# A gated mix of memory attention and a token MLP on one core: DMA issue moved off POOL, half of the LN apply moved to ACT, instruction order changed

## The chip, the cores and the metric

The kernel runs on one core of a Trainium2 chip. The time is the device time of one execution in microseconds (us).

Engines: PE (matmuls; PEld is its weight load), DVE (VectorE), ACT (ScalarE), POOL (GpSimd), SP (SyncE, which here only issues DMAs). "DMA on POOL" means that POOL's instruction stream starts the transfer.

## The reference

```python
x = A_x                                   # [1, 2048, 448] bf16, 16 heads of 28
g = sigmoid((x * gate_w).sum(-1))
# a: four stripes of 512 tokens; causal softmax attention inside a stripe, plus a
#    linear-attention memory (phi(q) M / phi(q) z) of the earlier stripes; then @ wo
# b: h = layernorm(x); u = gelu(h^T w1 + b1); y = u w2 + b2, mixing over the tokens
return g * a + (1 - g) * b                # [1, 2048, 448]
```

## The kernel before

A helper records every operation with the buffers that it reads and writes and derives the semaphore waits from that. One list gives the order; each engine executes its own entries of it, in that order. An entry is `what@engine`, with buffer or bank numbers after the engine (`P01`: PSUM banks 4 and 5).

```python
# the head of the list in the kernel before, line breaks added
warm@P ldwk.0@A dve0@D id@G ldx.0@S ldx.1@S ldwq.0@A ldsm@G ldwk.1@S acttab@A ldwq.1@S ldwv.0@S
trx.0.2@P xw.0@D  ... seven trx.0, seven trx.1 ...  setup@G ... ldwv.1@S ... ex.1@A ... ex.0@D pad.0@D ex.3@A
xtd.1@S ex.2@D tb@A bn.1@D pair.0.1@P01 pad.1@A bn.3@D bet@D pair.0.0@P23 eq.0.1@A btr@P1 ek.0.1@D ...
```

What the entries do, as far as the argument needs it:

```python
NWARM = 7                       # warm: dummy 128x512 matmuls at the start

def setup(eng, u):              # POOL
    op("POOL", lambda e: e.memset(mhalf[:], -0.5), writes=[R_mhalf])
    op("POOL", lambda e: e.memset(maskg[:], 0.0), writes=[R_maskg])
    op("POOL", lambda e: e.memset(oAM[:], 0.0), writes=R_o)          # 128 x 3072 bf16

def xw(eng, u, h):              # DVE: 64 columns of x copied behind the row, for the transposes
    op("DVE", lambda e: e.tensor_copy(x0[:, r, D:512], x0[:, r, 0:64]), ...)

# ldsm: five small loads (gate_w twice, b1, b2, beta).  ldx: x.  ldwk/ldwq/ldwv: weights, in halves.
# trx: PE transposes x of stripe 0.  ex: their copies out of PSUM.  pad: repack of wk and wq.
# pair.s.g: K and Q projection of stripe s, head group g (14 matmuls).  eq/ek: their evictions.
# v.p: V projection, its last column is the gate.  gt: tanh of the gate, on ACT.
# btr: transpose of gate_w, b1, b2 on PE; gcp, b1c, b2c: its copies.  tb, bet: sigmoid(beta), head masks.
# xtd, xtc, ldx.2: transposed and plain loads for stripe 1.
# sc/exp/mask/pv: scores, exponential, causal mask, P times V.  u, y: the two token matmuls of the MLP.
# bn, lnc: LN statistics.

def lna(eng, u, t):             # LN apply, on DVE
    op(eng, lambda e: e.tensor_scalar(xtile(t)[:, 0, :], xtile(t)[:, 0, :], rstd[:, t : t + 1],
                                      nmr[:, t : t + 1], op0=ALU.mult, op1=ALU.add), ...)
```

The softmax here doesn't subtract the row's maximum and nothing guards it: scores larger than these inputs give would overflow.

## Time and profile before

| | before |
|---|---|
| time, median of the first three runs | 190.9 us (189.59 to 190.95) |
| span of the profiled run | 188.6 us |
| PE busy | 175.7 us |
| PE idle before 33 us / in 33-67 us / in 67-186.1 us / after | 5.7 / 4.35 / 0.4 / 2.5 us |

The page's first part, two lines: the span, and PE's busy time, share and instructions.

```profile
span 188.6 us, 3618 instructions
...
PE 175.7 (93%) x1470; PEld 81.9 (43%) x1470; DVE 140.2 (74%) x271; ACT 122.2 (65%) x110; POOL 57.8 (31%) x94
```

The stretches view of the kernel before: each line is a stretch of time, its length, then busy time of each engine in it.

```profile
0.00:11.00 11.00, 6.33 (x35) 3.85 (x36) 7.42 (x11) 3.29 (x6) 6.75 (x14) 1.00 0.94 186
11.00:33.00 22.00, 20.99 (x191) 9.14 (x192) 20.07 (x55) 15.22 (x23) 9.70 (x28) 1.00 1.10 248
33.00:67.00 34.00, 29.65 (x276) 12.82 (x275) 30.39 (x57) 27.86 (x26) 13.27 (x25) 1.00 0.61 131
67.00:100.00 33.00, 32.91 (x312) 13.87 (x311) 26.35 (x47) 27.05 (x23) 10.65 (x11) 1.00 0.33 83
```

The first busy number is PE's, the third is DVE's. PE is nearly full from 67 us on; in 33-67 us it lacks 4.35 us while DVE is busy for 30.4 of 34 us.

The timeline of the kernel before at the start, in order of time (start, length, engine, line, operation; in brackets the idle time before it and what ended it):

```profile
1.45 1.30 POOL L356 DMA_DIRECT2D t<-in_gate_w_dram  x2
...
3.75 0.58 POOL L356 DMA_DIRECT2D t<-in_A_beta_dram  x1
...
4.12 3.49 DVE L508 COPY t<-t 128x128 bf16<-128x128 bf16 x2
...
4.27 1.27 PE L517 MATMUL t<-t 128*128 128x128 bf16 x10
...
4.84 2.68 POOL L443 MEMSET t<- 128x3072 bf16 x1
7.63 1.84 PEld L517 LDWEIGHTS t<-t 128*128 128x128 bf16 x18 [2.35 <-DVE t L508]
7.63 2.10 PE L517 MATMUL t<-t 128*128 128x128 bf16 x18 [2.08 <-DVE t L508]
...
11.00 4.62 PE L545 MATMUL t<-t 64*128 64x512 bf16 x28 [1.27 <-DVE t L366]
...
11.40 0.15 PEld L545 LDWEIGHTS t<-t 64*128 64x128 bf16 x2 [0.28 <-issue]
...
13.95 1.18 PEld L545 LDWEIGHTS t<-t 64*128 64x128 bf16 x12 [0.26 <-issue]
```

Two things are to be seen. The copies of x columns (L508) end with POOL's memset (at 7.6 and 7.52 us), and PE waits 2.08 us for them. And the first projections (L545) start slowly: until 13.95 us there is one step of weight loads in about 0.43 us, afterwards twelve loads in 1.18 us, which is one step of two in about 0.2 us. That is half the rate (the array is "cold" below; at full rate it is "warm"). The column for the granted clock (the 1.00 in the stretches) doesn't show it in this profile.

The source view of the LN apply on DVE (min/median/max ns), for its cost:

```profile
L833 DVE TENSOR_SCALAR t<-t x16: 307/386/1162, 23.3 to 46.5; 128x448 bf16<-128x448 bf16 x16
```

### The profile page before, as it was taken

To read this page: it belongs to the slowest core of one execution; us is meant where nothing else is said; L and a number is where in the kernel's file an instruction comes from. 1 tells how busy PE (TensorE), PEld (TensorE's weight loads), DVE (VectorE), ACT (ScalarE), POOL (GpSimd) and SP (SyncE) were. 2 spreads that over 40 slices of the span, in tenths; PEclk is the share of its full clock that TensorE was granted. 3 is DMA by queue.
4 is the path that set the end of the run, shared out by engine and by line. 5 is a ranking of instruction groups with operands and counts; after the bars stand their busy time and mean duration, and the time that the engine had idled before them with its cause. 6 is when DMAs were issued, how large, how long until landed. Compare 5 with 4: busy or idle time off the path is not lost.

```text
span 188.6 us, 3618 instructions
## 1 busy us (share of the span) xinstructions
PE 175.7 (93%) x1470; PEld 81.9 (43%) x1470; DVE 140.2 (74%) x271; ACT 122.2 (65%) x110; POOL 57.8 (31%) x94
## 2 busy tenths in 40 slices
PE   7578999977998799999999999999999999999994
PEld 3524444332344354444345444454444444555554
DVE  5697999997998793894996538299835998596032
ACT  3157569967796968888799956995775668401300
POOL 8501566637223133323320222301333423200000
DMA  6999999979047231572008330660534470638011
GB/s 154 212 202 266 289 200 267 153 181 264 6 133 168 37 78 33 165 215 72 0 0 222 104 95 1 197 195 0 168 103 129 123 214 25 168 95 225 27 49 50
DMA packets 50296, 24.92 MB, mean 132 GB/s; under 512 B 15016, under 2 KB 49896, under 8 KB 50280
## 3 DMA queue, kind: packets, MB, share of 16 engines
q1 hardware_dynamic: 49192, 24.23, 52.4%
q10 hardware_dynamic: 928, 0.46, 1.1%
q8 instruction: 11, 0.18, 0.4%
q0 software_dynamic: 160, 0.01, 0.1%
q14 instruction: 5, 0.04, 0.1%
HBM read 18.54 MB, written 1.84 MB: 108 GB/s over the span
## 4 chain that ended last, share of the span: by engine, by line
PE 66%; DVE 19%; POOL 4%; issue 3%; ACT 2%; DMA 2%; SPq 1%; DVEq 0%
PE t L898 21%; PE t L845 16%; PE t L545 8%; PE t L871 7%; PE t L694 4%; PE t L735 4%; PE t L570 4%; DVE t L366 3%; DMA t<-t 2%; DVE t L617 2%; DVE t L508 2%; DVE t L833 2%; POOL t L812 2%; DVE t L803 1%; DVE t L608 1%
## 5 line engine op out<-in xcount | busy, mean ns | idle before, releaser
L704 ACT ACTIVATE t<-t 128x2048 bf16<-128x2048 f32 x40 | 75.1, 1877 | 22.5 <-PE t L694 22.3
L717 POOL TENSOR_SCALAR_AFFINE_SELECT t<-t 128x1024 bf16<-128x1024 bf16 (+1 forms) x40 | 38.4, 963 | 87.6 <-ACT t L704 73.9
L845 PE MATMUL t<-t 128*128 128x448 bf16 x224 | 48.7, 354 | 1.8 <-DVE t L833 1.3
L898 PE MATMUL t<-t 128*128 128x448 bf16 (+1 forms) x238 | 45.8, 342 | 0.0
L545 PE MATMUL t<-t 64*128 64x512 bf16 x224 | 28.0, 392 | 3.4 <-DVE t L366 2.6
L898 PEld LDWEIGHTS t<-t 128*128 128x128 bf16 x238 | 22.3, 98 | 20.1 <-issue 2.5
L845 PEld LDWEIGHTS t<-t 128*128 128x128 bf16 x224 | 20.1, 98 | 24.4 <-issue 5.3
L364 ACT ACTIVATE t<-t 128x512 bf16<-128x512 f32 (+4 forms) x27 | 16.6, 636 | 12.6 <-PE t L517 5.0
L907 DVE SCALAR_TENSOR_TENSOR t<-t 128x448 bf16<-128x448 f32 (+1 forms) x17 | 11.0, 649 | 16.0 <-PE t L898 15.9
L545 PEld LDWEIGHTS t<-t 64*128 64x128 bf16 x224 | 10.6, 97 | 18.1 <-issue 4.4
L366 DVE CAST t<-t 128x512 bf16<-128x512 f32 (+1 forms) x24 | 15.4, 650 | 2.3 <-PE t L570 1.8
L694 PE MATMUL t<-t 28*128 28x512 bf16 (+3 forms) x256 | 15.8, 301 | 0.0
L871 PE MATMUL t<-t 128*128 128x448 bf16 x64 | 13.8, 353 | 0.0
L881 ACT ACTIVATE t<-t 128x448 bf16<-128x448 f32 x8 | 5.8, 722 | 11.8 <-DVE t L884 11.4
L613 ACT ACTIVATE t<-t 128x1024 bf16<-128x1024 bf16 x12 | 12.6, 1056 | 0.0
L570 PE MATMUL t<-t 64*128 64x449 bf16 x112 | 12.1, 350 | 0.0
L755 DVE STREAM_TRANSPOSE t<-t 128x512 f32<-128x512 f32 x16 | 11.0, 700 | 1.2 <-PE t L735 1.2
L735 PE MATMUL t<-t 128*32 128x512 bf16 (+3 forms) x256 | 11.1, 301 | 0.7 <-DVE t L366 0.4
L776 DVE SCALAR_TENSOR_TENSOR t<-t 128x448 bf16<-128x448 f32 x16 | 11.4, 724 | 0.2
L759 DVE STREAM_TRANSPOSE t<-t 128x512 f32<-128x512 f32 x12 | 8.4, 697 | 4.3 <-PE t L748 4.3
L795 DVE STREAM_TRANSPOSE t<-t 128x512 bf16<-128x512 bf16 x16 | 11.2, 698 | 0.1
L884 DVE TENSOR_SCALAR t<-t 128x448 bf16<-128x448 f32 x8 | 6.0, 744 | 6.8 <-PE t L871 6.7
(70 smaller groups left out, 157.8 us busy)
## 6 DMA issues: line engine op xcount, KB each, us to landing
t<-in_B_w_dram SPq DMA_DIRECT2D x7, 1024.0 KB, 6.4
t<-in_B_w_dram SPq DMA_DIRECT2D x8, 896.0 KB, 5.1
out_dram<-t SPq DMA_DIRECT2D x15, 112.0 KB, 1.7
t<-in_A_x_dram SPq DMA_DIRECT2D x3, 448.0 KB, 4.6
t<-t SPq DMA_DIRECT2D x6, 192.0 KB, 3.2
t<-in_A_wv_dram SPq DMA_DIRECT2D x2, 392.0 KB, 8.0
t<-in_A_x_dram SPq DMA_DIRECT2D x2, 224.0 KB, 3.7
t<-in_A_wo_dram SPq DMA_DIRECT2D x4, 98.0 KB
```

What stands on the lines that cost most here:

```text
L364: op("ACT", lambda e: e.activation(out, in_, ACT.Copy), reads=reads, writes=writes)
L366: op(eng, lambda e: e.tensor_copy(out, in_), reads=reads, writes=writes)
L545: last = e.matmul(bank(bb)[:, 0:512], wkq[half[h], c, 128 * hg : 128 * hg + 128], xTb[half[h], b, i, :], start=(i == 0), stop=(i == 6), sk ...
L570: last = e.matmul(bank(bs[h])[:, 0 : D + 1], xTb[half[h], b, i, k0 : k0 + 128], wvx[half[h], (LC, UC)[h][i], 0 : D + 1], start=(i == 0), s ...
L613: op("ACT", lambda e: e.activation(et[:, i, :].rearrange("p (g t) -> p g t", g=2), two(T, hp, s), ACT.Exp), reads=[RT[2 * hp][s], RT[2 * h ...
L694: last = e.matmul(bank(hl)[:, c0 : c0 + w], kT[r, hg, s * 512 + j * 128 : s * 512 + j * 128 + 128], qT[r, hg, s * 512 + 128 * j : s * 512 ...
L704: op("ACT", lambda e: e.activation(punit(i).rearrange("p (a q) -> p a q", a=4), ps[:, 0:4, :], ACT.Exp, scale=SCALE), reads=R_bank[0:4], w ...
L717: op("POOL", lambda e: e.affine_select(d, d, pattern=pat, compare_op=ALU.is_ge, fill=0.0, base=0, channel_multiplier=-1), reads=[R_P[i]], ...
L735: last = e.matmul(bank(b)[32 * hl : 32 * hl + 32, 128 * j : 512], vaug[:, 4 * s + j, 32 * h : 32 * h + 32], p4[:, hl, c0 : c0 + w], start= ...
L845: op("PE", lambda e: e.matmul(bank(b)[:, 0:D], w[:, st, (ft % 2) * 128 : (ft % 2) * 128 + 128], xtile(st)[:, 0, :], start=(st == 0), stop= ...
L871: last = e.matmul(bank(b)[:, 0:D], oT[:, hg, T * 128 : T * 128 + 128], wo_sb[:, hg, :], start=(hg == 0), stop=(hg == NHG - 1), skip_group_ ...
L898: op("PE", lambda e, b=b, f=f, c0=c0, n=n: e.matmul(bank(b)[:, 0:n], w[:, f, c : c + 128], uT[:, f, c0 : c0 + n], start=(f == 0), stop=(f ...
```

## The change

Its intent: POOL issues no DMA any more, so that its memsets come early; ACT issues the loads of wv; SP issues the small loads after x; the LN apply may run on DVE or ACT; the whole order was found anew by annealing, with instruction durations varied so that the order does not lean on exact ones. There is also one more warm-up matmul.

```diff
-NWARM = 7
+NWARM = 8
 PLAN = """
-warm@P ldwk.0@A dve0@D id@G ldx.0@S ldx.1@S ldwq.0@A ldsm@G ldwk.1@S acttab@A ldwq.1@S ldwv.0@S trx.0.2@P xw.0@D
-... setup@G trx.1.0@P ldwv.1@S ... tb@A bn.1@D pair.0.1@P01 pad.1@A bn.3@D bet@D pair.0.0@P23 eq.0.1@A btr@P1 ...
+warm@P ldwk.0@A dve0@D id@G ldx.0@S ldx.1@S ldwq.0@A setup@G ldsm@S ldwv.0@A ldwv.1@A acttab@A ldwk.1@S ldwq.1@S
+... pad.0@D tb@A bn.3@D pair.0.0@P01 bn.0@D bet@D btr@P2 eq.0.0@A ek.0.0@A pair.0.1@P31 b2c@D pad.1@A gcp@D ...
 ... (about 80 lines of order; LN applies 1,2,4,5,7,9,12,14 on ACT; two projections of stripe 2 much later)
     def lna(eng, u, t):
+        x, sc_, bi = xtile(t)[:, 0, :], rstd[:, t : t + 1], nmr[:, t : t + 1]
+        if eng == "ACT":
+            op("ACT", lambda e: e.activation(x, x, ACT.Identity, bias=bi, scale=sc_), ...)
+        else:
+            op(eng, lambda e: e.tensor_scalar(x, x, sc_, bi, op0=ALU.mult, op1=ALU.add), ...)
```

## The prediction

> **What bounds it now.** TensorE. The page's first part gives PE 175.7 us busy of a 188.6 us span. The stretches view places the 12.9 us of idle: 4.7 us before 11 us, 1.0 in 11-33, 4.35 in 33-67, 0.7 in 67-186.1, and the 2.5 us tail. After 67 us the order hardly matters; what can be won lies before.
>
> **The start.** The groups list DVE's copy of x columns (two pieces) at 3458 and 1743 ns; the timeline has them from 4.12 to 7.6 us, ending as POOL's 2.68 us memset (4.84-7.52) ends, and PE waits 2.1 us for them. [...] POOL is that late because it issues five small DMAs first (1.45-4.33 us). The first 14 column steps of the first projection take about 0.43 us each, until 13.95 us, so two projections take 4.62 us instead of about 3.2. [...]
>
> **What the change does.** POOL goes from the identity straight to its memsets (3.4 us), which should end near 4.8-5.0 us instead of 7.5. The x copies then end at 5-6 us, about 2 us earlier. The first projection should start at 9-9.3 us instead of 11.0, and nearer full rate: another 0.7-1.4 us. Against it: SP issues the small loads (about 0.6 us each, from its other issues; some 3 us), so the second halves of wk and wq leave near 5 us instead of 1.8-2.6, the x transposes about 1.5 us later, and ACT's wv loads compete. Later projections may wait briefly. Net gain by the first token-mixing matmul (32.6 us before): 2-3 us.
>
> **33-67 us.** DVE is 30.4 of 34 us busy there, and the chain of waits runs through DVE pieces from 35 to 57 us. The LN apply has median 386 ns but mean 534 and maximum 1162, again beside POOL. Eight move to ACT (about 0.55 us each, estimated from its 448-element evictions), taking about 4.3 us off DVE; two projections of stripe 2 with their evictions move later, which relieves both. Of the 4.35 us idle I expect 1.5-2.5 back. Four more output combines on DVE come late and cost nothing. PE's switches between kinds of work barely change (154 to 158 in the order).
>
> **Sum.** Gains 2-3 + 1.5-2.5 us, less about 0.5 us of new waits: 4.5 us, that is 186.3 us from 190.9. Range 183.5 to 189.6. Chances: faster by over 2% 0.60, within 2% 0.37, slower 0.03.
>
> **What would show it right.** POOL's long memset ends before 5.2 us and the x copies last under 1.5 us; the first projection starts before 9.7 us and the first two take under 4 us; PE idle before 33 us falls from 5.7 to about 3.5, in the next 34 us below 3; LN apply on DVE keeps a mean below 534 ns; PE busy falls by 1-1.5 us in total (less cold time); the rest stays PE-bound, same tail.
>
> **What would make it wrong.** DVE memsets or x copies still blocked by the earlier POOL memsets; the late wk and wq halves or stripe 1's transposes arriving after PE wants them (PE waits on the weight repack or DMA at 12-18 us); ACT becoming the limit at 20-45 us; holes in 50-100 us because filler work was spent early.

The copies end at 7.6 us as the memset does at 7.52, and the two projections take 4.62 us instead of about 3.2. The sum: 2-3 and 1.5-2.5 us, 5 us together in the middle, less 0.5 us make its 4.5 us.

Two remarks in it have these numbers in the traces. Its longest LN applies did run beside POOL: the one of 1162 ns at 44.64 us beside a mask of 44.55 to 45.68 us, the one of 1.14 us at 30.03 beside a mask of 29.95 to 31.05. That loads compete was its estimate: the DMA share was 0.94 and 1.10 in the first two stretches of before; in after the second halves of wk and wq landed 7.0 and 6.9 us after their issue, in before 5.8 us, and whether the wv loads caused that was not tested.

Two figures in it are misread: its "14 column steps" of about 0.43 us are 14 matmuls in seven pairs, 0.43 us a pair, and the stretches give 0.4 us of idle in 67-186.1 us, not 0.7.

## The result, and the profile after

| | before | after |
|---|---|---|
| time, median | 190.84 us (189.59 to 190.95, 4 runs) | 184.53 us (183.97 to 185.70, 4 runs) |
| ratio | 1 | 0.9692, 95% interval 0.9630 to 0.9753 |
| span of the profiled run | 188.6 us | 182.2 us |
| PE busy | 175.7 us | 172.7 us |
| PE idle before 33 us / in 33-67 us | 5.7 / 4.35 us | 6.3 / 0.5 us |

A ratio is the mean time of one kernel's fast runs over that of the other's of the same rounds, so it is not quite the ratio of the medians. The kernel is 3.1% faster.

The page's first part and the stretches of the kernel after:

```profile
span 182.2 us, 3611 instructions
...
PE 172.7 (95%) x1471; PEld 79.7 (44%) x1471; DVE 135.7 (74%) x268; ACT 123.9 (68%) x116; POOL 54.5 (30%) x89
...
0.00:11.00 11.00, 6.84 (x51) 3.36 (x51) 5.52 (x12) 3.20 (x6) 3.80 (x9) 1.00 0.96 190
11.00:33.00 22.00, 19.86 (x206) 8.09 (x206) 20.43 (x53) 20.93 (x30) 12.51 (x34) 1.00 1.02 215
33.00:67.00 34.00, 33.50 (x303) 14.69 (x300) 27.92 (x54) 29.01 (x30) 12.66 (x20) 1.00 0.90 182
67.00:100.00 33.00, 33.00 (x299) 14.58 (x298) 25.92 (x52) 27.84 (x27) 6.70 (x7) 1.00 0.24 65
```

The 6.4 us of span split into 3.0 us less PE busy time and 3.4 us less idle. The idle was won in 33-67 us (3.85 us). Before 33 us there is more of it than before (0.6 us). PE does the same matmuls in both kernels but for one warm-up, so busy time that vanishes is time in which the same matmuls ran slower: the transposes took 3.37 us and now take 1.89, the first two projections 4.62 and now 1.69 and 1.68.

The timeline of the kernel after, its start:

```profile
1.80 2.66 POOL L443 MEMSET t<- 128x3072 bf16 x1
...
4.10 0.41 DVE L508 COPY t<-t 128x128 bf16<-128x128 bf16 x1
4.38 0.94 PE L517 MATMUL t<-t 128*128 128x128 bf16 x14
...
5.65 0.19 DVE L508 COPY t<-t 128x128 bf16<-128x128 bf16 x1 [1.14 <-DMA t<-in_A_x_dram]
...
8.21 1.69 PE L545 MATMUL t<-t 64*128 64x512 bf16 x14 [1.58 <-DVE t L366]
10.82 0.19 PE L462 MATMUL t<-t 37*128 37x37 bf16 x1 [0.93 <-DMA t<-in_A_beta_dram]
...
11.55 1.68 PE L545 MATMUL t<-t 64*128 64x512 bf16 x14 [0.54 <-ACT t L364]
```

The memset now ends at 4.46 us; the copies take 0.6 us together; the first projection starts at 8.21 us instead of 11.0 and runs at full rate from its first step (14 matmuls in 1.69 us). But then PE waits for the small loads (beta landed at 10.8 us) and for ACT. The second projection begins at 11.55 us. So 2.8 us of an earlier start are there, and by 33 us PE has been idle for longer than before.

The LN apply after, on both engines:

```profile
L838 DVE TENSOR_SCALAR t<-t x8: 377/390/1240, 20.5 to 39.8; 128x448 bf16<-128x448 bf16 x8
...
L835 ACT ACTIVATE t<-t x8: 746/776/820, 20.9 to 39.3; 128x448 bf16<-128x448 bf16 x8
```

### The profile page after: what moved, and what is told of

It is laid out like the page before. It is cut to its first block, busy times and chain, and to the rows that moved or that the text cites. A ratio compares the mean times of both kernels' runs of the same rounds, so it can differ in the third digit from the quotient of the medians.

```text
span 182.2 us, 3611 instructions
## 1 busy us (share of the span) xinstructions
PE 172.7 (95%) x1471; PEld 79.7 (44%) x1471; DVE 135.7 (74%) x268; ACT 123.9 (68%) x116; POOL 54.5 (30%) x89
## 4 chain that ended last, share of the span: by engine, by line
PE 75%; SPq 6%; DVE 6%; ACT 5%; DMA 4%; POOL 1%; issue 1%
PE t L902 22%; PE t L849 21%; PE t L545 8%; PE t L875 7%; PE t L694 6%; SPq L356 6%; PE t L570 5%; PE t L735 4%; DMA t<-in_A_x_dram 4%; ACT t L704 3%; ACT t L835 2%; PE t L748 2%; PE t L659 1%; DVE t L366 1%; DVE t L803 1%
## 5 line engine op out<-in xcount | busy, mean ns | idle before, releaser
L545 PE MATMUL t<-t 64*128 64x512 bf16 x224 | 26.6, 377 | 3.3 <-DVE t L366 2.8
L364 ACT ACTIVATE t<-t 128x512 bf16<-128x512 f32 (+4 forms) x27 | 16.4, 644 | 5.0 <-PE t L545 2.2
L545 PEld LDWEIGHTS t<-t 64*128 64x128 bf16 x224 | 9.8, 94 | 16.9 <-DVE t L366 3.9
L885 ACT ACTIVATE t<-t 128x448 bf16<-128x448 f32 x4 | 2.9, 724 | 18.9 <-PE t L875 18.9
L755 DVE STREAM_TRANSPOSE t<-t 128x512 f32<-128x512 f32 x16 | 11.3, 709 | 5.0 <-PE t L735 5.0
L888 DVE TENSOR_SCALAR t<-t 128x448 bf16<-128x448 f32 x12 | 8.7, 728 | 6.3 <-PE t L875 6.3
L784 DVE TENSOR_TENSOR t<-t 128x448 bf16<-128x448 f32 x12 | 10.9, 911 | 0.1
L776 DVE SCALAR_TENSOR_TENSOR t<-t 128x448 bf16<-128x448 f32 x16 | 10.9, 687 | 0.1
```

What stands on the lines that cost most here:

```text
L364: op("ACT", lambda e: e.activation(out, in_, ACT.Copy), reads=reads, writes=writes)
L545: last = e.matmul(bank(bb)[:, 0:512], wkq[half[h], c, 128 * hg : 128 * hg + 128], xTb[half[h], b, i, :], start=(i == 0), stop=(i == 6), sk ...
```

## The experiments

Twelve runs were made (eleven edited kernels and the kernel after again), all with correct results. Line numbers of their profiles are mostly one lower than in the kernels that they were made from. An overview, each ratio against the kernel before in the same rounds.

| run | what it is | ratio | 95% interval |
|---|---|---|---|
| e1_memset_held | before, POOL's long memset out of the way of the x copies | 0.9903 | 0.9856-0.9949 |
| e2_new_front_old_order | new loads and start, old order and apply | 0.9974 | 0.9916-1.0033 |
| e4_old_front_new_order | old loads and start, new order and apply | 0.9855 | 0.9819-0.9892 |
| e3_apply_on_dve | after, all LN applies on DVE | 0.9710 | 0.9674-0.9745 |
| a1_after_again | after, unedited | 0.9679 | 0.9641-0.9717 |
| l1_apply_on_act_old_order | before, eight LN applies on ACT | 0.9938 | 0.9901-0.9974 |
| w16_before_sixteen_warm | before, 16 warm-up matmuls | 0.9858 | 0.9832-0.9884 |
| x16_old_front_new_order_warm | e4 with 16 warm-up matmuls | 0.9693 | 0.9671-0.9714 |
| i1_small_consumers_late | after, small loads used later | 0.9652 | 0.9615-0.9690 |
| i2_small_loads_last | i1, small loads issued later too | 0.9736 | 0.9701-0.9770 |
| i3_bet_on_pool | i1 mended, beta work on POOL | 0.9705 | 0.9669-0.9741 |
| i4_x_load_first | i3, one x load moved ahead | 0.9608 | 0.9587-0.9630 |

### Were the x copies held by POOL's memset?

```diff
 # kernel before; setup@G is moved behind pad.0@D in the list, and
-op("POOL", lambda e: e.memset(oAM[:], 0.0), writes=R_o)
+op("POOL", lambda e: e.memset(oAM[:], 0.0), reads=[R_wp[0]], writes=R_o)
```

> The kernel before, with one edit: POOL's three memsets are held back until the first weight repack on DVE has ended (a true dependence), so that none of them runs while the x columns are copied. POOL still issues the small loads. If the x copies lasted 3.4 us because POOL's long memset blocked DVE (my theory), they take under 0.7 us together, PE's wait of 2.1 us for them shrinks to at most 1.2 us (the arrival of the second x load), the first projection starts near 9 us and the time falls by 1 to 3 us. If they waited for the x loads instead (rival), they still take about 3 us and nothing moves.

The edit holds back less than this says: only the long memset waits, the two short ones still run at 4.34 to 4.93 us.

Measured: 0.9903, 189.1 us median. From the timeline of this run:

```profile
4.11 0.25 DVE L507 COPY t<-t 128x128 bf16<-128x128 bf16 x1
...
5.93 0.20 DVE L507 COPY t<-t 128x128 bf16<-128x128 bf16 x1 [1.57 <-DMA t<-in_A_x_dram]
5.96 0.96 PE L516 MATMUL t<-t 128*128 128x128 bf16 x14 [0.87 <-DMA t<-in_A_x_dram]
...
13.86 2.83 PE L544 MATMUL t<-t 64*128 64x512 bf16 x14 [0.69 <-ACT t L363]
```

The first copy takes 0.25 us instead of 3.46. The rival, that it waited for x, falls. So the long memset held the copies in this kernel; by what mechanism, the runs do not show. One thing stays open: by the records the long memset began at 4.84 us, while without it the first copy was over at 4.36 us, so its start time does not explain the hold (the profile itself calls spans on POOL rough). PE's wait was 0.87 us, within the expected 1.2, and the first projection started at 8.65 us.

The 0.9903 is not what the held copies are worth. The transposes and the first two projections of `e1` are warm (0.95 and 0.96 us for 14 each, then 3.19 us), but its third projection, at 13.86 us, and the V projection behind it are cold (2.83 us against 1.69, 2.08 against 1.50), after gaps of 1.14 and 0.69 us.

### Front and order apart

`e2` takes the kernel before and replaces only what stands ahead of the transposes:

```diff
-warm@P ldwk.0@A dve0@D id@G ldx.0@S ldx.1@S ldwq.0@A ldsm@G ldwk.1@S acttab@A ldwq.1@S ldwv.0@S ... setup@G ... ldwv.1@S
+warm@P ldwk.0@A dve0@D id@G ldx.0@S ldx.1@S ldwq.0@A setup@G ldsm@S ldwv.0@A ldwv.1@A acttab@A ldwk.1@S ldwq.1@S
-NWARM = 7
+NWARM = 8
```

`e4` is the reverse: these lines of the kernel before in the kernel after.

> The kernel before with only the loads and the start of the change: no DMA on POOL, its memsets right after the identity, wv loads on ACT, small loads on SP, eighth warm-up matmul; the order from the transposes on, and the LN apply, as before. If the front is worth what I predicted, 2 to 3 us faster than before (188 to 189 us), with the first projection near 8.3 us. If the whole gain of 6.3 us comes from the front (rival 1), 184 to 186 us. If the early start is given back in full to waits for the small loads and for the second weight halves (rival 2), within 1 us of before.

> The kernel after with the loads and the start of the kernel before (POOL issues the small loads, its memsets come last, wv on SP, seven warm-up matmuls), with the new order and the new LN apply. If the parts add up with the run that has only the new front, this is 3 to 4 us faster than before (187 to 188 us). If the new order needs the early start, it is no faster than before. The x copies should take about 3.4 us again and the first projection start near 11 us.

Measured: the new front alone gives 0.9974, not told apart from nothing. The order and the apply alone give 0.9855, 188.07 us. Together the two give 0.9692. The parts don't add: 0.3% and 1.45% against 3.1%.

The PE timelines of `e2` (first fence) and `e4` (second) tell why:

```profile
8.83 4.79 PE L544 MATMUL t<-t 64*128 64x512 bf16 x28 [2.12 <-DVE t L365]
```

```profile
10.57 3.17 PE L544 MATMUL t<-t 64*128 64x512 bf16 x14 [1.32 <-DVE t L365]
...
14.43 3.17 PE L544 MATMUL t<-t 64*128 64x512 bf16 x14 [0.67 <-ACT t L363]
```

At full rate 14 of these take 1.69 us and 28 take 3.19. In `e2` two projections took 4.79 us, in `e4` two took 3.17 us each. Both are still cold, though `e2` starts its first projection at 8.83 us. For `e4` the profile's page shows half clock outright, in its line for the granted clock (40 slices of 4.65 us, in tenths; 9 is 90% or more), with a 5 in the two slices from 9.3 to 18.6 us:

```profile
PEclk9855999999999999999999999999999999999999
```

So cold time, not the start time, looked like the missing piece. A theory from two profiles is not enough; the next runs test it.

### Cold time by itself

```diff
 # w16: the kernel before.  x16: e4 (old front, new order).  In both only:
-NWARM = 7
+NWARM = 16
```

The nine further dummy matmuls run while PE would wait for the x copies anyway: in `w16` the transposes begin at 7.74 us, and in the kernel before they resume at 7.63.

> The kernel before with sixteen warm-up matmuls instead of seven, nothing else: PE stays busy until about 6.3 us, inside the time in which it waits for the x copies anyway. If the cold stretch of before (about 2.9 us more for the transposes and the first two projections than in after) comes from PE's idle time before them, the two projections take about 3.2 us instead of 4.6 and the time falls by 1.5 to 3 us. If the cold stretch depends on the execution alone (rival), it stays within 0.7 us of before.

> The run with the old loads and the new order (188.07 us, about 4 us of cold time in its profile), with sixteen warm-up matmuls. Theory: the new front is worth little but the warm array, so this comes within 1 us of after: 184.3 to 185.6 us. Rival: the new front is worth its earlier first projection (2.4 us); then this stays 2 us or more behind after, at 186.5 us or more.

Measured: `w16` 0.9858, 188.19 us; `x16` 0.9693, 184.99 us. PE timelines of `w16` and then of `x16`:

```profile
1.31 6.59 PE L449 MATMUL t<-t 128*128 128x512 bf16 x16 [1.31 <-DVE t L927]
...
11.04 3.19 PE L545 MATMUL t<-t 64*128 64x512 bf16 x28 [1.57 <-DVE t L366]
...
15.02 1.69 PE L545 MATMUL t<-t 64*128 64x512 bf16 x14 [0.77 <-ACT t L364]
```

```profile
10.40 1.69 PE L544 MATMUL t<-t 64*128 64x512 bf16 x14 [1.58 <-DVE t L365]
...
12.78 1.69 PE L544 MATMUL t<-t 64*128 64x512 bf16 x14 [0.68 <-ACT t L363]
```

In `w16` the first projection starts no earlier than in the kernel before (11.04 against 11.00 us), and two projections take 3.19 us instead of 4.62. One constant, nine more dummy matmuls, is worth 1.4% or 2.7 us (0.0142 of 191 us). The rival, that the cold stretch depends on the execution alone, falls. The expectation missed one thing: the warm-ups ran until about 7.8 us, not 6.3, at about 0.41 us each.

The profiles place only part of the 2.7 us. Matmul by matmul, `w16` is 1.39 us ahead of the kernel before when the third projection starts (15.02 against 16.41 us), all of it from the first projection, and 1.78 us from 66 us on. The transposes, warm too (28 in 1.73 us, in before 3.37), gained nothing, since the first projection starts no earlier. The other 0.9 us is not located (the profiled `w16` is the slowest of its four).

`x16` keeps POOL's DMAs, its late memsets and the held x copies, starts its first projection 2.2 us later than after does, and is as fast as after (0.9693 against 0.9692 and, in the repeat, 0.9679). So within these intervals, and in the new order, the whole new front of the change is worth the warm array and nothing else. The new front with a warm array in the old order was not run. With a warm array the order and the apply give 0.9858 to 0.9693, that is 1.65% or about 3.1 us, and the sum of 2.7 and 3.1 us is the gain (5.9 us, 3.1% of 191).

### The LN apply

`e3` is the kernel after with the letter of eight list entries changed from A to D; `l1` is the kernel before with the new `lna` function and the same eight on ACT.

> The kernel after, with all sixteen LN applies on DVE again, order untouched. If moving half of them to ACT is what removed PE's idle time in 33-67 us (4.35 us before, 0.5 after), this is 2 to 4 us slower than after (186.5 to 188.5 us) with PE idle of over 2 us in that stretch. If the order did it (rival), it stays within 1 us of after.

> The kernel before with the same eight LN applies on ACT, order and loads untouched. If the relief of DVE by itself is worth the 1.5 to 2.5 us that I predicted for 33-67 us, 188.5 to 189.5 us. If it only helps together with the new order (which the small cost of undoing it there, about 1 us, already makes likely), within 1 us of before, since ACT then pays about 0.78 us for each and its exponentials come later.

Measured: 0.9710 and 0.9938. In the old order the move is worth 0.6% (about 1.2 us), more than nothing and less than the 1.5 to 2.5 us predicted for the relief. In the new order undoing it costs 0.2 to 0.3% (about 0.3 to 0.6 us, intervals overlapping with after's; by the medians 1.0 us, so the rival of `e3` holds narrowly). So most of the 3.1 us is the order. The stretch 33-67 us of `l1`, then of `e3`:

```profile
33.00:67.00 34.00, 31.40 (x292) 13.82 (x294) 28.31 (x54) 31.91 (x33) 14.47 (x29) 1.00 0.62 130
```

```profile
33.00:67.00 34.00, 32.80 (x299) 14.45 (x296) 28.27 (x60) 27.30 (x27) 14.34 (x24) 1.00 0.86 182
```

PE's idle time there is 4.35 us before, 2.6 with the apply alone, 1.2 with the order (and the new front) but not the apply, and 0.5 with all. The order relieves DVE there as much as the move does (28.3 us of DVE busy time in both, 30.4 before): two projections of stripe 2 with their evictions now come later. It also brings ACT's exponentials forward: the first starts at 13.62 us instead of 21.47. Both are seen in the profiles; which of the order's many moves brought the gain was not tested.

### What limits the start of the kernel after

`i1` moves the consumers of the small loads behind the second projection and gives that projection banks which it need not wait for; `i2` also issues the small loads after the second weight halves:

```diff
-... pad.0@D tb@A bn.3@D pair.0.0@P01 bn.0@D bet@D btr@P2 eq.0.0@A ek.0.0@A pair.0.1@P31 b2c@D pad.1@A gcp@D b1c@D bn.1@D bn.2@D sc.0.0@P
+... pad.0@D bn.3@D pair.0.0@P01 bn.0@D eq.0.0@A ek.0.0@A bn.1@D bn.2@D pair.0.1@P32 btr@P1 gcp@D tb@A sc.0.0@P ek.0.1@D eq.0.1@D b2c@D b1c@D bet@D pad.1@A
 # from there on PSUM banks 5 and 6 are exchanged
 # i2 only: ldsm@S stands behind ldwq.1@S
```

> The kernel after, unedited, as the anchor for the other runs of this call: 184 to 185.5 us. It also shows how much the cold time of the array changes from one execution to the next: if the cold stretch depends on the execution and not on the kernel, PE busy differs by about 1 us between this profile and the first one of after.

> The kernel after with the consumers of the small loads moved behind the second projection: PE's transpose of the biases, ACT's tanh of beta, DVE's use of both; the second projection in other PSUM banks, so that it waits for no eviction. In after, PE waits 0.93 us for the beta load and 0.54 us for ACT between the first two projections. If these waits are what ate the early start, the first V projection begins near 12.2 us instead of 13.6 and the time falls by 0.5 to 1.5 us against after. If DMA arrival of the second weight halves then binds instead (rival), PE waits move to the third projection and the time stays within 0.4 us of after.

> As the run before this, and SP issues the second halves of wk and wq before the five small loads instead of after them. If arrival of these halves (12.15 us in after) binds the second repack and with it the third projection, this is 0.3 to 1 us faster than the run before it. If the small loads then come so late that the V projection waits for the gate column, it is slower than that run.

Measured: `a1` 184.38 us median, but its profiled execution took 186.37 us; `i1` 184.43 us (0.9652, one of its six runs was slow and is left out); `i2` 185.83 us (0.9736), slower. `i1` is not told apart from after: the waits between the first two projections went, but PE then waited 1.3 us for the bias copies, so that the first V projection began at 14.00 us and not near 12.2, and 1.0 us for the gate's tanh. In `i2` beta landed at 13.2 us, PE waited 1.3 us for it, and one later projection ran cold (3.14 us). So, in this order, the small loads must stay early.

`a1` answers the question asked of it with no: its array was as warm as in the first profile (transposes 0.94 and 0.96 us, first two projections 1.68 and 1.69). Its slow execution has another cause, shown in its timeline:

```profile
22.06 1.16 DVE L803 BATCH_NORM_STATS2 t<-t 128x6 f32<-128x448 bf16 x2 [3.23 <-DMA t<-in_A_x_dram]
...
25.55 1.69 PE L545 MATMUL t<-t 64*128 64x512 bf16 x14 [2.17 <-DVE t L366]
```

DVE sat 3.23 us in front of the LN statistics, whose x tiles (the second x load) had not landed; the evictions queued behind them, and PE waited 2.17 us for an eviction. In the first profile of after DVE waited 1.0 us there.

`i3` mends what `i1` showed:

```diff
-pair.0.1@P32 btr@P1 gcp@D tb@A sc.0.0@P ek.0.1@D eq.0.1@D b2c@D b1c@D bet@D pad.1@A ... ev.2@D pke.0.0@A0 ev.3@D ... gt.1@A
+pair.0.1@P32 btr@P1 gcp@D b2c@D b1c@D tb@A sc.0.0@P ek.0.1@D eq.0.1@D pad.1@A ... lnc.0@G bet@G ... ev.2@D ev.3@D gt.1@A pke.0.0@A0
 # bet runs on POOL; the masks on POOL also wait for its last results
```

> As the run with the consumers of the small loads moved back, mended where its profile showed new waits: the three copies of the transposed biases right after it, the fourteen small beta instructions on POOL instead of DVE, the tanh of the gate before the exponential of the first key features. In that run PE waited 1.3 us for the bias copies and 1.0 us for the gate's tanh. If those waits are all that took the gain, the first V projection begins near 13 us, the fourth projection near 16.3 us instead of 17.9 to 18.4, and the time is 183 to 184 us. If stripe 1 or the LN statistics then wait for their DMAs (rival), within 0.5 us of after.

Measured: 184.98 us, 0.9705: no gain. The timeline of `i3`, PE and one line of DVE:

```profile
12.53 1.50 PE L569 MATMUL t<-t 64*128 64x449 bf16 x14
...
16.03 1.69 PE L544 MATMUL t<-t 64*128 64x512 bf16 x14
...
20.93 1.15 DVE L802 BATCH_NORM_STATS2 t<-t 128x6 f32<-128x448 bf16 x2 [2.88 <-DMA t<-in_A_x_dram]
...
24.42 1.69 PE L544 MATMUL t<-t 64*128 64x512 bf16 x14 [2.49 <-DVE t L365]
```

The V projection and the fourth projection came 1.1 and 1.9 us earlier than in after, as intended, and all of it was returned at 24.42 us: DVE had waited 2.88 us for the same x load. The rival holds.

`i4` moves that load. In `i3` SP issues it after the copies `xtc.1`, and SP waits for the transposed load before it can issue those (it stands idle from 12.35 to 14.18 us).

```diff
-pad.1@A xtc.1@S v.1@P01 lnc.0@G bet@G exp.0.0@A0 ldx.2@S
+pad.1@A ldx.2@S xtc.1@S v.1@P01 lnc.0@G bet@G exp.0.0@A0
```

> As the run with the beta instructions on POOL, and one DMA moved: SP issues the x tiles of stripe 1 (second x load) before the copies that wait for the transposes to land, where SP otherwise sits idle from 12.4 to 14.2 us. In that run DVE waited 2.9 us for these tiles (1.0 us in the first profile of after, 3.2 in its second) and PE then 2.5 us for DVE. If that load is what now limits the start, DVE's wait falls below 1 us, PE's waits in 16-26 us below 1 us in sum, and the time is 182 to 183.8 us: faster than after by 0.5 to 2 us. If the DMA queue as a whole limits it (rival), the copies of stripe 1 come later instead, PE waits for them, and the time stays at 184.5 to 185.5 us.

Measured: 183.69 us, all five runs within 183.60 and 183.82 us, ratio 0.9608 (0.9587 to 0.9630), below the intervals of `i3` (0.9669 to 0.9741), from which it differs by this one move, and of after's repeat (0.9641 to 0.9717); it overlaps with `i1`'s. DVE no longer waited for the moved load; 0.4 us of waiting, at 25.4 us, is for the x load after it. PE's waits, from the list of who waited for whom:

```profile
PE t L544 <- DVE t L365: 1.8, 1, 1.8
...
PE t L544 <- DMA t<-t: 1.1, 1, 1.1
PE t L544 <- ACT t L363: 0.6, 1, 0.6
```

The 1.8 us are those at 8.47 us, ahead of the first projection. In 16-26 us only 1.1 us are left (a bit more than expected), for the copies of stripe 1, which the moved load delayed, as the rival said. `i4` is the fastest of all kernels run, about 1 us ahead of after (means 183.70 and 184.72 us), a small step. It was run at another time. Its even times fit that the spread of after came from the late x load; other causes were not tested.

## Why the prediction was right, point by point

It said 186.3 us, faster by over 2% with a chance of 0.60, range 183.5 to 189.6. Measured was 184.53 us. The cause of its largest part was named, but its terms were mis-sized, and one of them was the wrong one.

- *PE bounds the kernel, only the time before 67 us can be won*: right. PE idle from 67 us to the tail went from 0.4 to 0.15 us and the 2.5 us tail stayed, so the gain lies before.
- *POOL's memset holds the x copies*: right, shown by `e1`. In after the copies fell to 0.41 and 0.19 us, the memset ended at 4.46 us, the first projection started at 8.21 us. All better than the signs asked for. It brought little by itself (next point).
- *"Net gain by the first token-mixing matmul: 2-3 us", made of about 2 us of earlier start and "another 0.7-1.4 us" of full rate*: the sum fits (2.7 us), the terms do not. The earlier start was worth nothing that the runs can show (`x16` equals after), and the warm array was worth all of it. That the sum fits is luck: in the old order the same front left the array cold and gave 0.3% (`e2`), and nothing in the prediction foresaw that the order decides this. In the profiles the cold excess in busy time was 1.5 us in the transposes (3.37 against 1.89 us), which I overlooked, and 1.4 us in the first two projections (4.62 against 3.2). `w16` shows the second part as time won and the first part not.
- *"PE idle before 33 us falls from 5.7 to about 3.5"*: wrong. It was 6.3 us, in `a1` 8.3 us. The named risk, waits for loads, came true, mostly with other loads than those named: the beta load (PE waited 0.93 us at 10.8 us) and later the second x load (DVE waited 1.0 us, in `a1` 3.2); for the second halves of wk and wq ACT's repack waited only 0.16 us. About 0.5 us had been set aside for all new waits. What the step missed: with PE ahead, loads and the work that waits for them set the pace until about 25 us (`a1`, `i3`, `i4`).
- *33-67 us gives 1.5-2.5 us back, through relief of DVE*: the direction was right, the size too small. PE idle there fell by 3.85 us, and with a warm array order and apply together gave 3.1 us. The order, not the apply, is the larger part.
- *An LN apply on ACT costs about 0.55 us*: too low, 0.776 us measured (746 to 820 ns). I had taken it from ACT's evictions of 448 elements, plain copies without per-partition scale and bias (L364, mean 549 ns in before). What makes the difference was not tested.
- *LN apply on DVE under a mean of 534 ns*: wrong, 584 ns (4.7 us over 8). Its median stayed 390 ns and its longest rose to 1240 ns.
- *PE busy falls by 1-1.5 us*: it fell by 3.0 us, the same mis-sized cold time.

What stays open: how much idle time in which arrangement cools the array. `e2` had only 2.12 us of idle before its cold projections and 1.6 us left other runs warm, but no run steps that length alone. It cannot be the length of the last gap alone, for in `e1` a projection ran cold after gaps of 1.14 and 0.69 us, and in `i4` one stayed warm after 1.85 us. And the 0.6% of the apply in the old order and the 0.2 to 0.3% in the new one overlap in their intervals.

## What to carry to other kernels

Before reordering a kernel's start, look at the step from one matmul to the next there: a cold array can hide in busy time (here two projections took 4.62 us instead of 3.19), and a few dummy matmuls placed in a wait that exists anyway may be worth as much as a reworked start (here nine gave 1.4%, and in the new order `x16` equals after). An engine or a load made earlier counts only as far as the next late load; find that one (here the second x load, behind a wait on the issuing engine; DVE waited 2.88 us for it in `i3`) before counting the gain. Read the granted clock over several executions, since a single 1.00 can hide half rate (here 0.43 us a step in before, under a reading of 1.00). To split a change into parts, run the parts both ways round, since here 0.3% and 1.45% made 3.1%.

## What the runs show of cold time and of late loads

- In `e2` the transposes ended at full rate (the last ten weight loads in 0.60 us), PE then idled for 2.12 us, and the next steps took 0.43 us each, at half rate, until about 12.2 us (granted clock 0.89 in 0-11 us, 0.98 in 11-33). In `e1` a projection ran cold after gaps of 1.14 and 0.69 us; with 1.57 to 1.85 us of idle before the first projection (`w16`, `x16`, `i4`) the array stayed warm (1.69 us for one projection, 3.19 for two). Avoiding the cold stretch of the kernel before gave 1.4%, 2.7 us (`w16`).
- The profile of the kernel before reads 1.00 in 11-33 us, while weight loads came only every 0.43 us until 13.95 us, and other executions of it read 0.97 to 0.98. The time from one matmul to the next was the sign to go by.
- The beta load came no earlier from SP than from POOL: it landed 6.9 us after its issue by POOL (before) and 7.2 us after its issue by SP (after), at 10.7 and 10.8 us. A wait on the issuing engine held back that engine's later load: in `i3` DVE waited 2.88 us for a load that SP issued at 15.39 us, behind copies that had to wait; issued ahead of them, at 13.07 us (`i4`), it was not waited for. (Between two executions of after this wait was 1.0 and 3.2 us, so one profile of each is weak; the times of `i3` and `i4` do not overlap.)
